# Moving key and value tiles to common places modulo 256, and weight sums forward in VectorE's order

## The chip, the core and the metric

The kernel runs on one core of a Trainium2 chip. The core has a matrix engine (TensorE, PE in the profile, with its weight loads as PEld), a vector engine (VectorE, DVE), an activation engine (ScalarE, ACT), GpSimd (POOL, nearly unused here) and a sync engine (SyncE, SP) that here issues almost all transfers between device memory and the on-chip memory. Engines run side by side; each takes its own instructions in the order in which they were written, and semaphores make one wait for another. The metric is the time of one execution on the device in microseconds (us), lower being better.

## The reference

Inputs are q, k and v, each [8 batches, 8 heads, 576 tokens, 64], and the weights of a channel mix. First attention, in chunks of 64 tokens:

```python
scores = scale * np.matmul(q_c, k_c.transpose(0, 1, 2, 4, 3))
scores = scores - np.max(scores, axis=-1, keepdims=True)
attn = np.exp(scores)
attn = attn / (np.sum(attn, axis=-1, keepdims=True) + 1e-09)
out = np.matmul(attn, v_c)
```

The heads are then laid side by side, which gives x, [8, 576, 512], and the channel mix follows (x_prev is x one token earlier, zero at the start of a batch):

```python
xk = mu_k * x + (1.0 - mu_k) * x_prev
xr = mu_r * x + (1.0 - mu_r) * x_prev
k = np.maximum(xk @ w_k, 0.0)
v = k * k @ w_v
r = 1.0 / (1.0 + np.exp(-(xr @ w_r)))
return (r * v).astype(np.float32)
```

w_k is 512 x 1024, w_v 1024 x 512, w_r 512 x 512.

## The kernel before

**Tiling.** The 8 x 576 = 4608 tokens are cut into 18 groups of 256. Groups 0 and 1, and the loading and splitting of the weights, are written out in START, one word per step; groups 2 to 17 follow the list GROUP, once per group g. Each matrix product of the channel mix is made from tensors split in a high and a low part, in three passes (high x high, high x low, low x high). In the texts three streams of matmuls are called after their steps:

- K (`moe_k`, L627; the matmul is at L636, tile pk): per group 4 blocks of 24 matmuls. The stationary tile is a 128x128 piece of w_k (wk0, wk1 for high and low), the moving tile 128x256 of xk (xkhi, xklo).
- R (`moe_r`, L682; L689, tile pr): 24 matmuls per group, stationary xr (xrhi, xrlo), moving 128x512 of w_r (wr0, wr1).
- V: up to group 3 `moe_v` (L708; L720, tile pv), stationary the squared activations kk, moving a quarter b of w_v, 128x256. From group 4 on `moe_halves` (L827; L910, tiles vx and vyz) makes the same in seven products of 12 matmuls in place of eight, with sums of quarters of w_v and sums of activations (ks); this needs the weight sums described below.

Beside these stand the small 64-wide matmuls of attention: scores (s, L1011), probabilities times values (xps, L1096), and the transposes of p (pt, L1078).

PE's order within a group from 4 on: K (4 blocks), pt, R, xps, the scores of the group after the next, V. Group 2 has scores ahead of its K and again at its end, so that the K of group 3 follows scores too; group 3 then has the order of the later groups.

**Attention for the next group** runs during K. On VectorE: maximum m (L1039), subtraction (L1045), the mix mr for R (L1158), the turns qT and kT (L386: 32x32 transposes of the loaded queries and keys of a later group, out of q_ring and k_ring), then sum z (L1052), two small steps, and the normalization of p (L1062), which pt on PE waits for. The exponential (L1048) is ScalarE's. Of the words of GROUP, `Sc` is this attention chain, `De` and `Dl` are the turns, `Mr`, `Md` and `Mk` the mixes, `Pq` the transposes and products with the values, `L4`, `Lm` and `Lv` the loads, `Z` and `H` the activation sums and their high parts, and `W` the seven products.

**The weight sums.** `split_weights` (L749) has in group 2 seven steps B.0 to B.6: B.0 takes two tiles of room (bs0, bs1) in the buffers that held the activations of an earlier group; B.1, B.2 and B.4 add the high and low parts of three quarters of w_v (128x1024, `total`), B.3, B.5 and B.6 subtract sums from each other (`less`). In group 3 B.0 and B.1 make one more sum and difference, and C.0, C.2 and C.4 copy three results to their high parts on ScalarE (L797), C.1, C.3 and C.5 make the low parts on VectorE (L801). Group 4 makes the fourth (E).

**Order.** Nothing is planned by a program: each word of START and GROUP issues its steps at its place, and so sets the order on every engine. A sign before a word limits it: `=` to group 2, `+` to the others, `!` and `~` to the last group or all but the last. A step already issued is passed over at a later word, so an unmarked word after an `=` word of the same name holds for the other groups alone.

**Loads.** SP issues the loads of q and k in pieces (L223), 16 for each of the two tensors and each half batch, then those of v (L201) and the stores of the output, all in one queue in the order of the words. In group 2 two half batches are loaded, after that one in some of the groups.

**Places.** On-chip tiles come from pools, which lie one behind the other in the order in which they are opened, from L110 on. All tiles of the large pools have a multiple of 256 bytes per partition, but the pools par (mu2), par_m (m) and par_z (z) have 64 bytes each, and the two x tiles 4160 each, so what stands behind them begins 64 later modulo 256 (128 behind both x tiles). Counted from the place of the identity tile (pool const, 512 bytes), the kernel before has, modulo 256: wr, xr (rp) and xk (kp) at 0, behind par_m wk and the quarters of w_v (wts) and one sum (tmp) at 64, behind par kk and ks (mx) at 128, behind par_z the rings, p, qT and kT (ld, att) at 192, and mo (which holds another of the sums) at 64.

Of the kernel before, what the change touches and what calls it, by code (L numbers as in the profile page):

```python
# [8 lines left out]
F32R = mybir.dt.float32r  # L9
# [7 lines left out]
P = 128  # L17
# [36 lines left out]


GROUP = """
=Nc.0 K0.0 =L4 Sc.0 Sc.1 K0.12 Mr.0 De.01 Lm Sc.2 K0.34 K1.0 K1.12 E.0 Mr.1 Sc.3456 Mr.2 K1.34 K2.0 K2.12 E.1 H.0 K2.34
K3.0 Pq.0 K3.12 Z.0 Pq.1 K3.34 Z.1 H.1 H.3 Z.2 H.4 Z.3 H.2 H.5 Z.456
R0.0 R1.0 Pq.2 +Nn.0 Lv Z.78 R0.1 R1.1 Pq.3 Pq.4 B.01 Md.0 Mk.0
V0 V1.0 W.0 W.1 W.2 !W.3 !W.4 W.5 W.6 W.7 Mk.1 C.0 C.2 C.4 W.8 B.2 Mk.2 B.3 =Dl.01 B.456 C.1 C.3 C.5 V1.12345678 W.9 W.10 W.12 W.11 ~W.3 ~W.4 W.13 W.14 W.15 W.16 =Nn.0  # L60
"""


# [18 lines left out]
def tile_chunk_attention_channel_mix(  # L82
# [13 lines left out]
    B_, H, S, D = q.shape  # L96
    DM, FF = w_k.shape
    w_k, w_v, w_r = (w.bitcast(I32) for w in (w_k, w_v, w_r))
    HP = H // 2
    NB = DM // P  # L100
# [6 lines left out]
    def pool(name, bufs=1):  # L107
        return ctx.enter_context(tc.tile_pool(name=name, bufs=bufs))

    const = pool("const")  # L110
    rp = pool("rp")
    kp = pool("kp")
    par_m = pool("par_m")
    wts = pool("wts")
    tmp = pool("tmp", 2)
    par = pool("par")
    mx = pool("mx")
    par_z = pool("par_z")
    ld = pool("ld")
# [133 lines left out]
        do(f_move, "A")  # L253


    wk = [wts.tile([P, NB, FF], F32R, name=f"wk{s}") for s in range(2)]
    wr = [rp.tile([P, NB, DM], F32R, name=f"wr{s}") for s in range(2)]
    HF, HD = NF // 2, DM // 2
    tok = slice(0, TT), slice(TT, G)
# [3 lines left out]
    B = {}  # L263
# [956 lines left out]
    with tc.manual_schedule():  # L1220
        for word in START.split():
            name, _, e = word.partition(":")
# [107 lines left out]
```

## Time and profile before

| what | value |
|---|---|
| median of three runs | 581.24 us (580.86 to 582.17) |
| profiled execution, its own time | 582.63 us |
| span of its instructions | 580.8 us |
| TensorE busy, share of the span | 570.2 us, 98% |
| VectorE busy | 456.7 us, 79% |
| ScalarE busy | 354.8 us, 61% |
| mean granted TensorE clock | 0.997 |
| one group in the middle (228.47 to 257.89) | 29.42 us |

Times in the profile count from the span's start; L636 is line 636 of the kernel. Matmuls are pipelined, so a single matmul's duration (281 ns) is longer than the step from one to the next; the paces in the texts are a stretch's length divided by its number of matmuls. The chain of waits follows the work that ended last back from the last instruction, at each step to what released it or to the instruction before it on the same engine; in order of time each row gives its start, its length and its work. In a timeline the bracket at the end of a row gives the engine's idle time before it and what ended it.

### The profile page before, as it was taken

To read this page: it belongs to the slowest core of one execution; us is meant where nothing else is said; L and a number is where in the kernel's file an instruction comes from. 1 tells how busy PE (TensorE), PEld (TensorE's weight loads), DVE (VectorE), ACT (ScalarE), POOL (GpSimd) and SP (SyncE) were. 2 spreads that over 40 slices of the span, in tenths; PEclk is the share of its full clock that TensorE was granted. 3 is DMA by queue.
4 is the path that set the end of the run, shared out by engine and by line. 5 is a ranking of instruction groups with operands and counts; after the bars stand their busy time and mean duration, and the time that the engine had idled before them with its cause. 6 is when DMAs were issued, how large, how long until landed. Compare 5 with 4: busy or idle time off the path is not lost.

```text
span 580.8 us, 15342 instructions
## 1 busy us (share of the span) xinstructions
PE 570.2 (98%) x6497; PEld 541.9 (93%) x6497; DVE 456.7 (79%) x753; ACT 354.8 (61%) x530; POOL 0.7 (0%) x6
## 2 busy tenths in 40 slices
PE   8899999999899999999999999999999999999997
PEld 7789999999799999999999999999999999999997
DVE  1699898749789788878887878888888787977835
ACT  4799875453639292929293838383847474747562
POOL 0000000000000000000000000000000000000000
PEclk9899999999999999999999999999999999999999
DMA  9997152443543434340234333344333311111011
GB/s 288 221 315 184 46 111 75 87 70 64 107 105 61 97 57 99 56 101 1 75 52 103 60 88 60 69 87 79 78 73 77 70 49 38 37 38 37 2 37 37
DMA packets 184276, 49.25 MB, mean 85 GB/s; under 512 B 169608, under 2 KB 176272, under 8 KB 184208
## 3 DMA queue, kind: packets, MB, share of 16 engines
q1 hardware_dynamic: 183904, 48.01, 36.5%
q8 instruction: 51, 0.84, 0.6%
q10 hardware_dynamic: 304, 0.27, 0.1%
q14 instruction: 17, 0.14, 0.1%
HBM read 38.80 MB, written 9.44 MB: 83 GB/s over the span
## 4 chain that ended last, share of the span: by engine, by line
PE 91%; DVE 3%; SPq 3%; ACT 1%; DMA 1%; issue 0%; DVEq 0%
PE pk L636 33%; PE pr L689 16%; PE vx L910 14%; PE vyz L910 10%; PE pv L720 6%; SPq L223 3%; PE xps L1096 3%; PE s L1011 2%; PE pt L1078 2%; PE warm L1225 1%; PE trq L367 1%; PE trk L367 1%; PE s L410 1%; PE mxk L580 1%; PE mxr L580 1%; DMA k_ring<-in_k 1%
## 5 line engine op out<-in xcount | busy, mean ns | idle before, releaser
L636 PE MATMUL pk<-xkhi,wk 128*128 128x256 f32 x1152 | 206.1, 281 | 0.0
L636 PEld LDWEIGHTS pk<-xkhi,wk 128*128 128x128 f32 x1152 | 178.4, 189 | 0.3
L636 PE MATMUL pk<-xklo,wk 128*128 128x256 f32 x576 | 161.4, 280 | 0.0
L636 PEld LDWEIGHTS pk<-xklo,wk 128*128 128x128 f32 x576 | 108.2, 188 | 0.1
L656 ACT ACTIVATE rr<-pk 128x512 f32<-128x512 f32 x56 | 33.0, 590 | 107.9 <-PE pk L636 107.7
L689 PE MATMUL pr<-wr,xrhi 128*128 128x512 f32 x288 | 90.4, 395 | 0.0
L910 PE MATMUL vx<-b,ks 128*128 128x256 f32 x504 | 64.0, 276 | 0.0
L910 PE MATMUL vyz<-b,kk 128*128 128x256 f32 x504 | 64.0, 276 | 0.0
L689 PEld LDWEIGHTS pr<-wr,xrhi 128*128 128x128 f32 x288 | 52.7, 188 | 10.2
L910 PEld LDWEIGHTS vx<-b,ks 128*128 128x128 f32 x504 | 60.3, 188 | 0.0
L910 PEld LDWEIGHTS vyz<-b,kk 128*128 128x128 f32 x504 | 60.2, 188 | 0.0
L689 PE MATMUL pr<-wr,xrlo 128*128 128x512 f32 x144 | 56.2, 390 | 0.0
L720 PE MATMUL pv<-b,kk 128*128 128x256 f32 x384 | 45.0, 277 | 0.0
L720 PEld LDWEIGHTS pv<-b,kk 128*128 128x128 f32 x384 | 44.1, 188 | 0.2
L939 ACT ACTIVATE u<-vx 128x256 f32<-128x256 f32 x28 | 10.8, 384 | 50.7 <-PE vx L910 50.7
L747 DVE TENSOR_TENSOR kk<-rr,kk 128x1024 fp32r<-128x1024 f32 x28 | 33.1, 1223 | 10.4 <-ACT kk L894 10.3
L747 DVE TENSOR_TENSOR xklo<-mk,xkhi 128x1024 fp32r<-128x1024 f32 x15 | 18.4, 1225 | 23.6 <-ACT xkhi L1168 23.6
L663 ACT ACTIVATE rr<-rr 128x512 f32<-128x512 f32 x56 | 35.4, 633 | 1.8
L689 PEld LDWEIGHTS pr<-wr,xrlo 128*128 128x128 f32 x144 | 27.0, 188 | 5.7
L1158 DVE SCALAR_TENSOR_TENSOR mk<-d,mu,x 128x256 f32<-128x256 f32 (+3 forms) x80 | 27.7, 413 | 0.4
L1158 DVE SCALAR_TENSOR_TENSOR mr<-d,mu,x 128x256 f32<-128x256 f32 (+3 forms) x80 | 27.6, 412 | 0.0
L856 DVE TENSOR_TENSOR ss<-rr 128x512 f32<-128x512 f32 x14 | 9.7, 692 | 21.8 <-ACT rr L663 21.8
(130 smaller groups left out, 885.5 us busy)
## 6 DMA issues: line engine op xcount, KB each, us to landing
v<-in_v SPq DMA_DIRECT2D x144, 64.0 KB, 2.4
out<-sg SPq DMA_DIRECT2D x34, 256.0 KB, 2.4
q_ring<-in_q SPq DMA_DIRECT2D x192, 36.0 KB, 2.0
k_ring<-in_k SPq DMA_DIRECT2D x192, 36.0 KB, 2.1
wk_st<-in_moe_w_k SPq DMA_DIRECT2D x4, 1024.0 KB, 12.7
wv_st<-in_moe_w_v SPq DMA_DIRECT2D x4, 1024.0 KB, 7.3
wr_st<-in_moe_w_r SPq DMA_DIRECT2D x2, 1024.0 KB, 10.0
q_ring<-in_q SPq DMA_DIRECT2D x2, 512.0 KB, 6.7
```

The costliest lines, as they stand in the source:

```text
L223: nc.sync.dma_start(out=ring[nm][pp : pp + 32, hp, a : a + n, :], in_=src[b, j * HP + hp, t0 : t0 + n * 32, dh * 32 : (dh + 1) * 32].rearr ...
L367: nc.tensor.matmul(x[halves[j], hp, :], T[f"{nm}{g}"][:, j * HP + hp, r, :], ident, start=True, stop=True,)
L580: nc.tensor.matmul(m[:, cb, s : s + w], diag[nm, n][:, cb], x[:, cb, c0 : c0 + w], start=(n == 0), stop=(n == 1),)
L636: nc.tensor.matmul(pk[:, e, :], wk[a][:, cb, f * P : (f + 1) * P], xk[b][:, cb, :], start=(n == 0), stop=(n == 3 * NB - 1),)
L656: nc.scalar.activation(r, T[f"pk{g}{fp}"], AF.Relu)
L663: nc.scalar.activation(r, r, AF.Square)
L689: nc.tensor.matmul(pr, xr[a][:, cb, tl * TT : (tl + 1) * TT], wr[b][:, cb, :], start=(n == 0), stop=(n == 3 * NB - 1),)
L720: nc.tensor.matmul(T[f"pv{g}{tl}"][:, cols[c]], kk[a][:, f, tok[tl]], quarter(f // HF, c)[:, b, f % HF, :], start=(f == 0 and n == 0 and c ...
L747: nc.vector.tensor_tensor(to, x, y, ALU.subtract)
L910: nc.tensor.matmul(to, a[i][:, f, :], weight(w, j, f), start=first and f == 0 and n == 0, stop=f == HF - 1 and n == 2, skip_group_check=True,)
L1096: nc.tensor.matmul(T[f"xps{g}"][halves[c], 2 * j + a, tl * TT + e * CH : tl * TT + (e + 1) * CH], T[f"v{2 * g + tl}"][halves[j], hp, e, :] ...
L1158: nc.vector.scalar_tensor_tensor(out=to[:, cb, s : s + w], in0=T[f"d{g}"][:, cb, s : s + w], scalar=mu[:, cb : cb + 1], in1=T[f"xg{g}"][:, ...
```

## The change

Two things. The pools are opened in another order: par stands first behind const, par_m moves behind tmp, and wk gets a pool of its own, wkp, between par_m and mx. In the same count as above, wr and xr come to lie at 64, xk at 64, the quarters and sums of w_v stay at 64, wk comes to 128, kk and ks stay at 128, and everything from par_z on stays where it was modulo 256.

| stream | stationary, moving before | stationary, moving after |
|---|---|---|
| K | wk 64, xk 0 | wk 128, xk 64 |
| V | kk or ks 128, weights 64 | kk or ks 128, weights 64 |
| R | xr 0, wr 0 | xr 64, wr 64 |

In GROUP, the weight sums of group 2 move forward: B.0 to B.2 behind the third K block's steps, B.3 to B.5 behind the x copy (Pq.4), B.6 behind the mix for K (Mk.0). In group 3 C.0 and C.1 move forward to the third K block, C.2 and C.4 behind Pq.4, C.3 and C.5 behind Mk.0. The number of instructions on each engine stays.

```diff
 GROUP = """
-=Nc.0 K0.0 =L4 Sc.0 Sc.1 K0.12 Mr.0 De.01 Lm Sc.2 K0.34 K1.0 K1.12 E.0 Mr.1 Sc.3456 Mr.2 K1.34 K2.0 K2.12 E.1 H.0 K2.34
+=Nc.0 K0.0 =L4 Sc.0 Sc.1 K0.12 Mr.0 De.01 Lm Sc.2 K0.34 K1.0 K1.12 E.0 Mr.1 Sc.3456 Mr.2 K1.34 K2.0 K2.12 E.1 H.0 K2.34 =B.012 C.01
 K3.0 Pq.0 K3.12 Z.0 Pq.1 K3.34 Z.1 H.1 H.3 Z.2 H.4 Z.3 H.2 H.5 Z.456
-R0.0 R1.0 Pq.2 +Nn.0 Lv Z.78 R0.1 R1.1 Pq.3 Pq.4 B.01 Md.0 Mk.0
-V0 V1.0 W.0 W.1 W.2 !W.3 !W.4 W.5 W.6 W.7 Mk.1 C.0 C.2 C.4 W.8 B.2 Mk.2 B.3 =Dl.01 B.456 C.1 C.3 C.5 V1.12345678 W.9 W.10 W.12 W.11 ~W.3 ~W.4 W.13 W.14 W.15 W.16 =Nn.0
+R0.0 R1.0 Pq.2 +Nn.0 Lv Z.78 R0.1 R1.1 Pq.3 Pq.4 C.24 =B.345 B.01 Md.0 Mk.0 =B.6 C.35
+V0 V1.0 W.0 W.1 W.2 !W.3 !W.4 W.5 W.6 W.7 Mk.1 W.8 Mk.2 =Dl.01 V1.12345678 W.9 W.10 W.12 W.11 ~W.3 ~W.4 W.13 W.14 W.15 W.16 =Nn.0
 """
...
     const = pool("const")
+    par = pool("par")
     rp = pool("rp")
     kp = pool("kp")
-    par_m = pool("par_m")
     wts = pool("wts")
     tmp = pool("tmp", 2)
-    par = pool("par")
+    par_m = pool("par_m")
+    wkp = pool("wkp")
     mx = pool("mx")
     par_z = pool("par_z")
...
-    wk = [wts.tile([P, NB, FF], F32R, name=f"wk{s}") for s in range(2)]
+    wk = [wkp.tile([P, NB, FF], F32R, name=f"wk{s}") for s in range(2)]
```

## The prediction

> **What bounds the kernel now.** I began with the busy time of each engine and the shares of the chain of waits by line.
>
> ```profile
> PE 570.2 (98%) x6497; PEld 541.9 (93%) x6497; DVE 456.7 (79%) x753; ACT 354.8 (61%) x530; POOL 0.7 (0%) x6
> PE pk L636 33%; PE pr L689 16%; PE vx L910 14%; PE vyz L910 10%; PE pv L720 6%; SPq L223 3%; PE xps L1096 3%; PE s L1011 2%; PE pt L1078 2%; PE warm L1225 1%; PE trq L367 1%; PE trk L367 1%; PE s L410 1%; PE mxk L580 1%; PE mxr L580 1%; DMA k_ring<-in_k 1%
> ```
>
> TensorE sets the time: its lines make nearly all of the chain. A wait elsewhere counts only where it stops PE, so two things are worth reading: how fast the matmul streams step, and where PE stands still. For the first, the chain in order of time (start, length, what; K is pk at L636, R is pr at L689, V is pv at L720 or vx and vyz at L910):
>
> ```profile
> 64.40 5.46 PE pr L689 x24
> 69.87 8.48 PE pk L636 x72
> 78.35 8.17 PE pv L720 x72
> ...
> 105.53 1.09 PE s L1011 x64
> 106.62 11.10 PE pk L636 x96
> ...
> 169.81 11.31 PE pk L636 x96
> ...
> 197.87 1.36 PE vx L910 x12
> 199.23 11.31 PE pk L636 x96
> ...
> 551.25 11.31 PE pk L636 x96
> 562.56 5.47 PE pr L689 x24
> 568.03 1.38 PE vx L910 x12
> ```
>
> K and V have one shape, a stationary 128x128 and a moving 128x256 tile, but not one pace. V steps by 1.36 / 12 = 113.3 ns; K from group 4 on by 11.31 / 96 = 117.8 ns. Yet K can step like V. The next rows are K's instructions alone in two stretches of 9 us (the number in brackets after PE's busy time counts its matmuls):
>
> ```profile
> 138.00:147.00 9.00, 9.00 (x82) 9.00 (x81) 1.00 0.38 75
> 171.00:180.00 9.00, 9.00 (x78) 9.00 (x78) 1.00 0.41 106
> ```
>
> PE is full in both at the full clock (the 1.00), with the same tiles at the same places; group 3 gets 82 matmuls through, group 4 78, 5% apart. So there are a quick pace and a slow pace, and what came before decides between them. K is quick where the 64-wide score matmuls (s) precede it, at 106.62, and slow where V precedes it without a break (the 14 blocks from 169.81 to 551.25, one a group), and where R does (69.87). V keeps its quick pace across seven products a group, though the product, the PSUM tile and the weights change at each: there the places modulo 256 stay. At V to K they change.
>
> The second thing, PE at rest, is in group 3. The same chain there, and VectorE's order just before it:
>
> ```profile
> 139.29 3.29 DMA k_ring<-in_k
> 142.67 1.67 DVE mr L1158 x4
> 144.33 1.16 DVE qT L386
> 145.49 1.13 DVE kT L386
> 147.19 1.14 DVE z L1052
> 148.85 1.24 DVE p L1062
> 150.13 1.09 PE pt L1078 x8
> ```
>
> ```profile
> 136.06 1.18 DVE L766 TENSOR_TENSOR bs<-b 128x1024 f32<-128x1024 f32 x1
> 137.27 2.49 DVE L747 TENSOR_TENSOR bs<-bs,bs 128x1024 f32<-128x1024 f32 x2
> 139.68 0.68 DVE L734 TENSOR_TENSOR sg<-pv,sg 128x512 f32<-128x512 f32 x1
> 140.28 1.21 DVE L1039 TENSOR_REDUCE m<-s 128x16 f32<-128x1024 f32 x1
> ```
>
> PE's last K matmul of group 3, and the same place in group 4, where nothing is late:
>
> ```profile
> 148.12 0.28 PE L636 MATMUL pk<-xkhi,wk 128*128 128x256 f32 x1
> ```
>
> ```profile
> 180.84 0.29 PE L636 MATMUL pk<-xkhi,wk 128*128 128x256 f32 x1
> 180.97 0.49 PE L1078 MATMUL pt<-ident,p 128*128 128x128 f32 x3
> ```
>
> In group 4 the transposes start 0.13 us after the last K matmul, in group 3 2.01 us after (150.13 - 148.12): 1.88 us of PE at rest, because VectorE normalizes p late. The maximum m needs only the scores, which PE makes just before K: K ends at 148.12 + 0.13 = 148.25 and takes 11.10 after scores (106.62), so they are done at 137.15. Three weight sums and an output scaling still stood in front of m then.
>
> **The change, part by part.** The execution profiled took 582.63 us (span 580.8), 1.39 above the median 581.24 of the three runs shown; the sum is a difference, taken from both.
>
> *Places.* Counted from the identity tile's place, the pools' sizes give, modulo 256: now K 64 stationary and 0 moving, V 128 and 64, R 0 and 0. Afterwards K and V are both 128 and 64, and R 64 and 64. The distance within K (64) and within R (0) stays. What goes is the change of place between V and K: the array sees V's pattern run on. I take it that K then stays in V's pace: 11.31 - 96 x 1.36 / 12 = 0.43 us a block, and 14 x 0.43 = 6.0 us. Bounds: 0, if the break at V to K has another cause, to 6.0; no loss, since no K row shows a pace below 118.
>
> If distance decides and not the place itself, two quick spells are lost. V at 78.35 steps by 8.17 / 72 = 113.5 ns though K before it was slow (8.48 / 72 = 117.8): the change of place brought it there, and will be gone. 72 x 4.3 ns = 0.31 us. The last V (84 matmuls from 568.03) is quick straight after R, with a place step of 128 for the stationary tile and 64 for the moving one; afterwards the step is today's from R to K, which leaves K slow at 69.87. 84 x 4.45 ns = 0.37 us. I count both as lost; bounds 0 and 0.68 together.
>
> R I leave at 5.47 / 24 = 228 ns: both operands share one place before and after. Bounds: the two paces of K differ by 4.45 ns, and 432 R matmuls at that are 1.9 us of gain; upward the slowest R row,
>
> ```profile
> 44.33 2.95 PE pr L689 x12
> ```
>
> is 246 ns, 18 ns more, or 7.8 us.
>
> A page of the Trainium skill speaks against this whole part: TensorE: Matmul & The Clock Gate (Part 2, What happens when you issue a matmul) gives PE two independent read ports and says that loading the next weights takes no read bandwidth from the running matmul. By that rule no placement could change the pace, and the 6.0 us would be 0. The two 9-us rows speak against its completeness, since one pair of tiles has two paces, but they don't name the cause; the rule has its own rival below.
>
> *Group 2's sums.* All seven steps (a reservation, six sums) move ahead on VectorE; none issues a DMA, and SP's order stays. Two sums go in before the last kk low part of K, three behind the x copy, one behind mk. Places with room, VectorE first and then ScalarE:
>
> ```profile
> 126.26 1.23 DVE L747 TENSOR_TENSOR d<-x 128x1024 f32<-128x1024 f32 x1 [3.90 <-ACT x L1122]
> ...
> 164.41 0.69 DVE L734 TENSOR_TENSOR sg<-pv,sg 128x512 f32<-128x512 f32 x1 [2.52 <-PE pv L720]
> ```
>
> ```profile
> 161.92 1.06 ACT L1168 ACTIVATE xkhi<-mk 128x1024 fp32r<-128x1024 f32 x1 [2.98 <-DVE mk L1158]
> ```
>
> Three sums are 3 x 1.22 = 3.7 us in VectorE's 3.90 us of waiting for x; without that cover each would delay x's difference by 1.2 us, which K needs only 137.15 - 126.26 = 11 us later. With them gone, m starts at about 137.25, when the scores end, and not at 140.28. What is late next? m and the subtraction take 142.67 - 140.28 = 2.39 and mr 1.66, so mr is done by 141.3, but the turns qT and kT stand ahead of z, and kT waits for the last keys to land at 139.29 + 3.29 = 142.58. That DMA is paced by SP's issues, which nothing here moves. So kT runs from 142.65 to about 143.8, not to 146.6. Then comes kk's low part, for which ScalarE must be done:
>
> ```profile
> 143.81 0.62 ACT L143 ACTIVATE kk<-relu 128x512 fp32r<-128x512 f32 x1
> ```
>
> That ends at 144.43; z follows 0.57 us later (146.62 to 147.19 now), and from z to the end of p it takes 148.85 + 1.24 - 147.19 = 2.90. So p is ready at 147.9, and PE wants it at 148.25. The 1.88 us go whole, with some 0.3 us to spare; bounds 0 (the landing a little later, or the turn's wait taking mr's place) to 1.88.
>
> *Group 3's splits.* C.3 and C.5 (2 x 1.22) go into VectorE's 2.52 us before the first scaling, C.2 and C.4 (two copies of the shape of xkhi's 1.06) into ScalarE's 2.98 us before xkhi, C.0 and C.1 beside K's end, where both engines wait for each other. Cost 0; uncovered they would delay xkhi and so K of group 4 by what exceeds these rests, under a microsecond.
>
> *Who covers the shorter K?* p must be normalized before K ends. The tightest group is 4:
>
> ```profile
> 179.07 1.23 DVE L1062 TENSOR_TENSOR p<-p,z 128x1024 f32<-128x1024 f32 x1
> ```
>
> It ends at 180.30 against 180.97. A K shorter by 0.43 leaves 0.24 us, so the gain reaches the end.
>
> **Sum.** 6.0 + 1.88 - 0.31 - 0.37 = 7.2 us: 582.63 becomes 575.4, and the median 581.24 becomes 574.0.
>
> **The rivals.**
>
> *The pace doesn't follow the places.* PE may lose its step at V to K for another reason (another weight matrix, another PSUM pool). For it: K is slow after R too (69.87). Against: V changes both at every product and keeps its pace. Then only the rest goes: 581.24 - 1.88 = 579.4. The Trainium skill's rule of two independent ports (TensorE: Matmul & The Clock Gate, Part 2) leads to the same time.
>
> *The keys land too late.* The wait for the DMA takes the place of the sums, and PE rests as long as now: 574.0 + 1.88 = 575.9. For it: the chain names this DMA. Against: VectorE had no rest between 142.67 and p's end.
>
> *Neither part does anything*: 581.2.
>
> *The other side: R pays.* R's 432 matmuls, whose two operands lie together, move to place 64, where K's stationary tile lies now while it is slow. If the place itself hurts and not the distance, K need not gain, and R at its slowest row costs 7.8: 581.24 - 1.88 + 7.8 = 587.2. It ends slower than before from (1.88 + 1.16) / 432 = 7 ns a matmul on. Against: V's moving tile has been at 64 all along, quick.
>
> *More than I count.* The early K and V blocks that are slow (24 + 72 + 24 + 18 = 138 matmuls, 0.6 us) come into step, the 0.68 isn't lost, and R gains its 1.9: 574.0 - 3.2 = 570.8.
>
> **How the numbers follow.** My forecast has 0.62, own range 573.3 (none of the 0.68 lost) to 574.9 (half of the 1.88 left); the unchanged pace 0.13; the late keys 0.08; neither 0.07; R pays 0.05; more 0.05. The range 572.6 to 579.8 holds the forecast, the late keys and the unchanged pace, 0.83. A difference of 0.2% (1.16 us) is about what three runs tell from none: faster 0.62 + 0.13 + 0.08 + 0.05 = 0.88, same 0.07, slower 0.05.
>
> **What would show it.** Right: the 14 K rows near 10.9 us and not 11.31; pt of group 3 starting within 0.2 us of the last K matmul; m of that group near 137.3; R still 5.47. Half right: K rows of 11.3, or a pt wait on p that stays. Wrong: R rows above 5.6, V rows above 1.40, or a new wait of PE in groups 4 to 17.

## The result and the profile after

The changed kernel takes 585.48 us (median of six runs, 584.55 to 586.69), the kernel before beside it 581.13 (580.85 to 582.64). The ratio is 1.007, with a 95% interval of 1.0051 to 1.0089: slower by 0.7%, where 574.0 had been forecast. The execution profiled took 586.23 us, its span is 584.5. The executions of one kernel fall into two sets about 2 us apart, here 584.55 to 584.81 at a mean granted clock of 0.999 or 1.000 and 586.16 to 586.69 at 0.997, so a kernel executed once is compared below only with executions at its own clock.

The busy line of the changed kernel's page:

```profile
PE 575.3 (98%) x6497; PEld 547.4 (94%) x6497; DVE 456.9 (78%) x753; ACT 354.3 (61%) x530; POOL 0.7 (0%) x6
```

PE is busy for 5.1 us more than before (575.3 against 570.2) with the same 6497 matmuls, and the rest of its span shrinks from 10.6 us to 9.2. So PE doesn't wait more; its matmuls step more slowly. The chain in order of time says which (start, length, work; lines after the change are one higher than before, so K is L637, R L690, V L721 and L911):

```profile
77.97 8.48 PE pv L721 x72
...
106.54 11.10 PE pk L637 x96
...
125.08 11.51 PE pv L721 x96
136.59 1.09 PE s L1012 x64
137.68 11.08 PE pk L637 x96
...
149.63 5.48 PE pr L690 x24
...
168.65 11.31 PE pk L637 x96
...
196.99 1.41 PE vx L911 x12
198.40 11.31 PE pk L637 x96
...
554.51 11.31 PE pk L637 x96
565.81 5.47 PE pr L690 x24
571.28 1.41 PE vx L911 x12
```

K behind V is 11.31 as before, in all 14 blocks; no gain there. V has lost its quick pace in every group from 2 on: a product takes 1.41 where it took 1.36 (117.5 ns a matmul, not 113.3, which within the rounding of the row is the 117.8 of K), the undivided V of groups 2 and 3 takes 11.51, and the early V at 77.97 takes 8.48 where the one at 78.35 took 8.17. K behind the scores (106.54, 137.68) is still quick. R still takes 5.47 or 5.48.

In group 3 the rest of PE is gone. VectorE there, and PE's last K matmul with the transposes behind it, as timelines of the changed kernel:

```profile
136.62 0.69 DVE L735 TENSOR_TENSOR sg<-pv,sg 128x512 f32<-128x512 f32 x1 [2.62 <-PE pv L721]
137.75 1.23 DVE L1040 TENSOR_REDUCE m<-s 128x16 f32<-128x1024 f32 x1 [0.43 <-PE s L1012]
...
142.89 1.20 DVE L387 STREAM_TRANSPOSE kT<-k_ring 128x1024 f32<-128x1024 f32 x1
...
147.18 1.22 DVE L1063 TENSOR_TENSOR p<-p,z 128x1024 f32<-128x1024 f32 x1
```

```profile
148.48 0.28 PE L637 MATMUL pk<-xkhi,wk 128*128 128x256 f32 x1
148.60 0.82 PE L1079 MATMUL pt<-ident,p 128*128 128x128 f32 x6
```

The maximum m starts at 137.75, 0.07 after the scores end (136.59 + 1.09 = 137.68). p is ready at 148.40, and pt starts at 148.60, 0.12 after the last K matmul. The sums' part of the change worked; the places' part cost more than it saved.

### The profile page after: what moved, and what is told of

Its sections match the earlier page's. It is cut to its first block, busy times and chain, and to the rows that moved or that the text cites. A ratio compares the mean times of both kernels' runs of the same rounds, so it can differ in the third digit from the quotient of the medians.

```text
span 584.5 us, 15341 instructions
## 1 busy us (share of the span) xinstructions
PE 575.3 (98%) x6497; PEld 547.4 (94%) x6497; DVE 456.9 (78%) x753; ACT 354.3 (61%) x530; POOL 0.7 (0%) x6
## 4 chain that ended last, share of the span: by engine, by line
PE 97%; DVE 2%; ACT 0%; issue 0%
PE pk L637 35%; PE pr L690 17%; PE vx L911 14%; PE vyz L911 10%; PE pv L721 8%; PE xps L1097 3%; PE s L1012 2%; PE pt L1079 2%; PE warm L1226 1%; PE trq L368 1%; PE trk L368 1%; PE s L411 1%; PE mxk L581 1%; PE mxr L581 1%; PE pt L475 0%; PE xps L495 0%
## 5 line engine op out<-in xcount | busy, mean ns | idle before, releaser
L637 PE MATMUL pk<-xkhi,wk 128*128 128x256 f32 x1152 | 206.4, 281 | 0.0
L637 PEld LDWEIGHTS pk<-xkhi,wk 128*128 128x128 f32 x1152 | 177.8, 189 | 0.3
L637 PE MATMUL pk<-xklo,wk 128*128 128x256 f32 x576 | 161.5, 280 | 0.0
L637 PEld LDWEIGHTS pk<-xklo,wk 128*128 128x128 f32 x576 | 108.3, 188 | 0.1
L657 ACT ACTIVATE rr<-pk 128x512 f32<-128x512 f32 x56 | 32.9, 588 | 113.3 <-PE pk L637 113.2
L690 PE MATMUL pr<-wr,xrhi 128*128 128x512 f32 x288 | 90.4, 395 | 0.0
L911 PE MATMUL vyz<-b,kk 128*128 128x256 f32 x504 | 66.2, 281 | 0.0
L911 PE MATMUL vx<-b,ks 128*128 128x256 f32 x504 | 66.2, 281 | 0.0
L911 PEld LDWEIGHTS vyz<-b,kk 128*128 128x128 f32 x504 | 62.4, 189 | 0.0
L911 PEld LDWEIGHTS vx<-b,ks 128*128 128x128 f32 x504 | 62.4, 189 | 0.0
L690 PEld LDWEIGHTS pr<-wr,xrhi 128*128 128x128 f32 x288 | 52.7, 188 | 10.1
L690 PE MATMUL pr<-wr,xrlo 128*128 128x512 f32 x144 | 56.1, 390 | 0.0
L721 PE MATMUL pv<-b,kk 128*128 128x256 f32 x384 | 46.2, 281 | 0.0
L721 PEld LDWEIGHTS pv<-b,kk 128*128 128x128 f32 x384 | 45.2, 189 | 0.2
L690 PEld LDWEIGHTS pr<-wr,xrlo 128*128 128x128 f32 x144 | 27.0, 188 | 5.7
```

The lines of the kernel that those rows point to most:

```text
L637: nc.tensor.matmul(pk[:, e, :], wk[a][:, cb, f * P : (f + 1) * P], xk[b][:, cb, :], start=(n == 0), stop=(n == 3 * NB - 1),)
L657: nc.scalar.activation(r, T[f"pk{g}{fp}"], AF.Relu)
L690: nc.tensor.matmul(pr, xr[a][:, cb, tl * TT : (tl + 1) * TT], wr[b][:, cb, :], start=(n == 0), stop=(n == 3 * NB - 1),)
L721: nc.tensor.matmul(T[f"pv{g}{tl}"][:, cols[c]], kk[a][:, f, tok[tl]], quarter(f // HF, c)[:, b, f % HF, :], start=(f == 0 and n == 0 and c ...
L911: nc.tensor.matmul(to, a[i][:, f, :], weight(w, j, f), start=first and f == 0 and n == 0, stop=f == HF - 1 and n == 2, skip_group_check=True,)
```

## The experiments

The theory on record is that a change of place between two streams changes their pace. The first rival is that each stream's pace comes from its own two places or the distance between them; the second that only the address far away counts (the weights of K moved by tens of thousands of bytes too); the third that no place matters. Places are again given modulo 256 as stationary/moving. The paces of a block of V from group 4 on are told by one product of 12 matmuls (1.36 or 1.41 us), those of K by its 96 (10.88 or 11.31). Ratios are against executions of the kernel before taken beside each run; where no ratio is given, the kernel was executed once and is read by its rows.

**The two parts one by one.** First the order alone, with the old places:

```diff
-=Nc.0 K0.0 ... H.0 K2.34
+=Nc.0 K0.0 ... H.0 K2.34 =B.012 C.01
...
-... Pq.4 B.01 Md.0 Mk.0
+... Pq.4 C.24 =B.345 B.01 Md.0 Mk.0 =B.6 C.35
```

> The order of the weight sums alone, the pools as before. If the two parts of the change are independent, as I hold: the rest of PE in group 3 goes (1.88 us, the transposes start within 0.2 us of the last K matmul), V stays at 113.3 ns and K at 117.8 ns, and the time falls by 1.9 us, to about 579.2 us. If the order itself had upset V's pace (because something now runs beside the start of V), V would be at 117.8 ns here too and the time about 585 us.

Measured: 579.53 us, ratio 0.9968 (0.9952 to 0.9984). The chain of waits of this run:

```profile
53.80 8.38 PE pk L636 x72
...
165.64 11.31 PE pk L636 x96
...
185.32 1.57 PE vx L910 x12
186.89 1.36 PE vyz L910 x12
```

The paces are those of before, and PE's rest in group 3 is gone. 0.32% of 581.98 is 1.9 us (0.9 to 2.8), against 1.88 in the forecast.

Then the places alone, with the old order:

```diff
     const = pool("const")
+    par = pool("par")
     rp = pool("rp")
     kp = pool("kp")
-    par_m = pool("par_m")
     wts = pool("wts")
     tmp = pool("tmp", 2)
-    par = pool("par")
+    par_m = pool("par_m")
+    wkp = pool("wkp")
...
-    wk = [wts.tile(
+    wk = [wkp.tile(
```

> The pools alone, the order as before. If the places alone set V's pace: V at 117.8 ns from group 2 on, K unchanged at 117.8 ns after V, the rest of PE in group 3 stays at about 1.9 us, and the time is about 587.3 us. If the order upsets V: the time of the kernel before, 581.1 us.

Measured: 587.47 us, ratio 1.0107 (1.0072 to 1.0142), V at 1.41 from group 4 on and K at 11.31. The two ratios multiplied give 1.0075, the whole change 1.007. All that is lost lies in the places. One detail differs: the last V, behind R, was quick here (its products take 1.36 or 1.37) and slow in the whole change, with the same places and the same order on PE.

**Far address or near place, and whose.** Next the weights of K went behind those of V, with no place modulo 256 changed: the quarters of w_v then lie exactly where the change puts them, the weights of K 64 bytes short of it. Then only the inputs moved (wr, xr and xk by 64), with the weights of K where they were:

```diff
     par = pool("par")
+    wkp = pool("wkp")
     mx = pool("mx")
...
-    wk = [wts.tile(
+    wk = [wkp.tile(
```

> The kernel before with one edit: wk gets its pool behind tmp, so that the quarters b of w_v move down by 32768 bytes to exactly where the change puts them, and wk up by 49152. No tile changes its place modulo 256 (K 64 and 0, V 128 and 64, R 0 and 0). Far-place theory (b and kk meet according to address bits above 256): V slow, 117.8 ns in every group, time about 587 us. Near-place theory (the places modulo 256 decide, those of the streams before V included): V quick, 113.3 ns, time about 581 us.

```diff
     const = pool("const")
+    par = pool("par")
     rp = pool("rp")
     kp = pool("kp")
-    par_m = pool("par_m")
     wts = pool("wts")
     tmp = pool("tmp", 2)
-    par = pool("par")
+    par_m = pool("par_m")
```

> The kernel before with the other half: par first and par_m behind tmp, so that wr, xr and xk move up by 64 bytes and wk, b, kk and ks stay where they were before. Modulo 256: K 64 and 64, R 64 and 64, V 128 and 64. Far-place theory: V quick, 113.3 ns; K may change, since its two tiles now share a place. Near-place theory: V slow as in the changed kernel, time about 587 us if K stays.

With the weights down: 580.66 us, ratio 0.9994 (0.9976 to 1.0013), every pace as before. The far address doesn't count. With the inputs up: 590.99 us, ratio 1.0168 (1.0139 to 1.0196): V slow although none of its tiles had moved, and K, with both tiles at 64, at 11.52 for 96 matmuls, 120.0 ns each, a third pace. So V's loss comes from the place of another stream's tiles, R's or K's.

**R's tiles or K's.** The runs up to the extra matmuls ahead of K stand on the order alone (579.53 us). First wr and xr at 64, the rest at the old places; then only xk at 64:

```diff
     const = pool("const")
-    rp = pool("rp")
     kp = pool("kp")
-    par_m = pool("par_m")
+    par = pool("par")
+    rp = pool("rp")
     wts = pool("wts")
     tmp = pool("tmp", 2)
-    par = pool("par")
+    par_m = pool("par_m")
```

> All four of these runs stand on the kernel of the order alone (579.5 us, V 113.3 ns, K 117.8 ns after V). Here only R's two tiles, wr and xr, move up by 64; K stays at 64 and 0, V at 128 and 64. If R's places decide how the V that follows two small streams later starts: V 117.8 ns as in the changed kernel, about 585.7 us. If K's places decide that: V stays at 113.3 ns, 579.5 us.

```diff
     rp = pool("rp")
+    par = pool("par")
     kp = pool("kp")
-    par_m = pool("par_m")
     wts = pool("wts")
     tmp = pool("tmp", 2)
-    par = pool("par")
+    par_m = pool("par_m")
```

> Only K's moving tile xk moves up by 64, so that K's two tiles share a place; R stays at 0 and 0. If R's places decide V's start: V 113.3 ns; K at 120 ns as in the run that moved all inputs up, about 582.6 us. If K's places decide it: V 117.8 ns, about 588 us.

The chain with R's tiles up:

```profile
178.86 5.49 PE pr L689 x24
...
187.98 1.41 PE vyz L910 x12
...
196.47 10.90 PE pk L636 x96
```

The chain with K's input up:

```profile
191.45 1.36 PE vyz L910 x12
...
199.61 11.52 PE pk L636 x96
```

It is R. With R at 64/64, R itself takes about as long as ever (5.49), V is slow, and K, at its old places 64/0 behind the slow V, is quick (10.90). That gain of K's was not expected, and so the 585.7 us expected for a slow V didn't come: 579.02 us were measured, at a clock of 1.000, where the order alone takes 578.35 to 578.60. What V loses K nearly gains back. With K's input up, V is quick and K at 120.0 ns, the slowest pace of K in any run. The 586.0 us are more than the 582.6 expected, in part because this execution had a clock of 0.997, and for the rest because K is that slow behind scores too (11.71 for 96, where it was 11.10) and the early K and V blocks are slower as well.

Does it take both of R's tiles? Once xr alone went to 64, once wr alone:

```diff
     const = pool("const")
-    rp = pool("rp")
+    wrp = pool("wrp")
     kp = pool("kp")
-    par_m = pool("par_m")
+    par = pool("par")
+    rp = pool("rp")
...
-    wr = [rp.tile(
+    wr = [wrp.tile(
```

> Only R's stationary tile xr moves up by 64: R's two tiles no longer share a place. If sharing a place costs a stream (K went from 117.8 to 120 ns when its tiles shared one): R falls from 227 ns by 2 ns or more, about 0.9 us in all, and if V keeps its pace the time is 578.6 us or less. If R is bound by its 512 columns and not by place: R 227 ns. V: quick if R's shared place is harmless to V whatever it is, slow if any move of R's tiles upsets it.

```diff
     rp = pool("rp")
     kp = pool("kp")
-    par_m = pool("par_m")
+    par = pool("par")
+    wrp = pool("wrp")
...
-    wr = [rp.tile(
+    wr = [wrp.tile(
```

> The order alone, and of the old places only R's moving weights move, from 0 to 64 (R's stationary inputs stay at 0). With both of R's tiles at 64 V was slow, with the stationary alone at 64 it was quick. If R's moving tile decides, V is slow here (9.88 us for the 84 products); if it is both tiles together, V is quick (9.52). R itself: near 235 ns as with the other tile moved, if the distance counts, near 232 otherwise. K is free to change, as it did before with R moved. Time 579 to 586.

The chain with xr alone at 64 (582.03 us, ratio 1.0006, 0.9973 to 1.0039), and then with wr alone (580.32 us):

```profile
180.54 5.60 PE pr L690 x24
...
189.75 1.36 PE vyz L911 x12
...
197.91 11.31 PE pk L637 x96
```

```profile
178.60 5.51 PE pr L690 x24
...
187.71 1.36 PE vyz L911 x12
...
195.88 11.31 PE pk L637 x96
```

V stays quick with either from group 2 on (the last V, with wr alone up, is slow: 1.41 a product). R itself is slower with its tiles apart: 0.13 us a group with xr moved, 0.04 with wr moved, which is 1.8 and 0.6 us over 14 groups. The expectation that R might gain 2 ns a matmul with its tiles apart is refuted: R's two tiles at one place cost R nothing. Of the three runs with tiles of R at 64, only that with both there upsets V in the groups from 2 on.

**Is the pace a property or a choice made at the start?** Ahead of K in groups 4 to 16 stood one extra matmul whose moving tile grows from group to group; its result is overwritten by the next, so no result changes and K starts otherwise than before:

```diff
             xk = T[f"xk{g}"]
+            many = (16, 32, 48, 64, 80, 96, 112, 128, 144, 160, 192, 224, 256, 0)[g - 4] if g >= 4 and fp == 0 else 0
+            if many:
+                nc.tensor.matmul(
+                    pk[:, 0, :many], wk[0][:, 0, 0:P], xk[0][:, 0, :many],
+                    start=True, stop=True, skip_group_check=True,
+                )
             for e in range(2):
```

> No place changes. Each K of groups 4 to 16 begins with one matmul more, whose result the first true one overwrites: the moving tile has 16, 32, 48, 64, 80, 96, 112, 128, 144, 160, 192, 224 and 256 columns in groups 4 to 16; group 17 has none. If the quick and the slow pace are two states of one stream, chosen by the offset between weight load and matmul at its start: for some of the sizes K runs at 113.3 ns from there on (10.9 us a group), for the others at 117.8. If the pace belongs to K's tiles after V: 117.8 ns in every group, and about 0.11 us more for each, 581 us.

The chain's K rows of groups 6, 7 and 11 (48, 64 and 128 columns):

```profile
224.49 11.39 PE pk L642 x96
254.03 10.98 PE pk L642 x96
...
370.50 11.36 PE pk L642 x96
```

The rows are up to 0.10 longer than without the extra matmul, but the two paces stand clear of each other: K is quick with 64, 80, 96, 112, 192 and 224 columns and slow with 16, 32, 48, 128, 144, 160 and 256 (577.61 us in all). The same tiles at the same places take either pace, for a whole block, by how the block starts. One size in all groups makes a kernel of it:

```diff
             xk = T[f"xk{g}"]
+            if g >= 4 and fp == 0:
+                nc.tensor.matmul(
+                    pk[:, 0, :80], wk[0][:, 0, 0:P], xk[0][:, 0, :80],
+                    start=True, stop=True, skip_group_check=True,
+                )
```

> The order alone (the old places), with an extra 80-column matmul ahead of K in groups 4 to 17, the size that made K quick in group 8 of the run with varied sizes. State theory: all 14 K blocks at 113.4 ns, each about 0.29 us shorter with the extra matmul counted, so 579.5 - 14 x 0.29 = 575.4 us, less than both kernels. If the quick K of that run hung on its group and not on the extra matmul's size, some groups stay at 117.7 and the time stays between 576 and 580.

Measured: 576.56 us (574.65 to 576.69), ratio 0.9904 (0.9877 to 0.993), and in each of the 14 groups the same row:

```profile
168.11 10.97 PE pk L641 x96
...
545.65 10.97 PE pk L641 x96
```

It is the size and not the group. One matmul more in each group makes the kernel faster than the kernel before and than the changed one.

**V's pace, and what K does behind it.** The same with the whole change: an extra matmul ahead of V, of the same sizes:

```diff
+            many = (16, 32, 48, 64, 80, 96, 112, 128, 144, 160, 192, 224, 256, 0)[g - 4]
+            if many:
+                nc.tensor.matmul(
+                    X()[:, :many], part(0, 0)[0][:, 0, :], weight(11, 0, 0)[:, :many],
+                    start=True, stop=True, skip_group_check=True,
+                )
             product(X(), part(0, 0), 11, True)
```

> The changed kernel with one extra matmul ahead of V in groups 4 to 16, of 16, 32, 48, 64, 80, 96, 112, 128, 144, 160, 192, 224 and 256 moving columns (its result is overwritten; group 17 has none). If V's slow pace in the changed kernel is a state chosen as the stream starts, some of the 13 blocks go back to 113.3 ns (the 84 fresh products then take 9.52 us and not 9.88) and the others stay at 117.8, as K did in the run with extra matmuls ahead of K. If it is a property of R's new place, all 13 stay at 117.8. K, which follows V, may change with it. Time by the state theory about 583 to 586; by the other 586 to 587.

The chain in group 8 (80 columns) and in group 12 (144):

```profile
309.53 1.36 PE vyz L911 x12
...
317.69 10.88 PE pk L637 x96
...
426.02 1.41 PE vyz L911 x12
...
434.50 11.31 PE pk L637 x96
```

V is quick with 80, 96, 112, 128, 192 and 224 columns and slow with the other seven, and K behind it has V's pace in all 13 groups: 10.88 behind a quick V, 11.31 behind a slow one (583.31 us). With K at V's places, K does take over V's pace. One size for all groups:

```diff
+            nc.tensor.matmul(
+                X()[:, :80], part(0, 0)[0][:, 0, :], weight(11, 0, 0)[:, :80],
+                start=True, stop=True, skip_group_check=True,
+            )
             product(X(), part(0, 0), 11, True)
```

> The changed kernel with an extra 80-column matmul ahead of V in groups 4 to 17. If R's place harmed V by the moment at which V starts and not by anything that lasts, all 14 V and all 14 K blocks are quick: a group is shorter by 29.76 - 29.12 = 0.64 us with the extra matmul counted, 585.5 - 14 x 0.64 = 576.5 us. If the quick groups of the earlier run hung on their predecessors, it stays between 578 and 586.

Measured: 578.01 us, ratio 0.9933 (0.9906 to 0.996). All V and K blocks from the extra matmul on are quick, but for the K of group 4, which follows the V of group 3, that has none:

```profile
167.19 11.31 PE pk L637 x96
...
188.54 1.36 PE vyz L911 x12
...
196.70 10.88 PE pk L637 x96
```

**The change with R left where it was.** If R alone stands between the change and its gain, one line is to be turned:

```diff
     const = pool("const")
-    par = pool("par")
     rp = pool("rp")
+    par = pool("par")
     kp = pool("kp")
```

> The changed kernel with one pool line moved: R's two tiles are back at place 0 and 0, K stays at V's places (stationary 128, moving 64), V as always. In every run so far with V at 128 and 64 and R's weights at place 0, V came quick out of the scores; in the changed kernel with an extra matmul ahead of V, K took over V's pace, quick or slow, in all 13 groups. If both hold, V is quick (9.52 us for the 84 fresh products, start to last) and K after it too (10.77 us for 96, not 11.19): 579.5 of the order alone less 14 x 0.42 = 573.6 us, below both kernels, and the forecast of 574.0 was right but for R. Rival: K's new place itself makes V or K slow: V 9.88 or K 11.19 stay and the time is 579 to 586.

Measured: 574.02 us (572.68 to 574.95), ratio 0.9875 (0.9848 to 0.9901). Its chain:

```profile
76.18 8.48 PE pv L721 x72
...
155.00 11.09 PE pv L721 x96
166.09 10.88 PE pk L637 x96
177.85 5.45 PE pr L690 x24
185.32 1.57 PE vx L911 x12
186.90 1.36 PE vyz L911 x12
...
195.06 10.88 PE pk L637 x96
...
566.26 1.37 PE vx L911 x12
```

V is quick, K behind it is quick, with no matmul added. This is the best of the kernels run: 1.25% below the kernel before, while the change as given is 0.7% above it, and 64 bytes of place of two tiles of R lie between them.

**The moment of R, or its address?** On the order alone, an extra matmul ahead of R in groups 4 to 16, so that R's start and length change and no place does:

```diff
+            many = (16, 32, 48, 64, 80, 96, 112, 128, 144, 160, 192, 224, 256, 0)[g - 4] if g >= 4 and tl == 0 else 0
+            if many:
+                nc.tensor.matmul(
+                    pr[:, :many], xr[0][:, 0, 0:TT], wr[0][:, 0, :many],
+                    start=True, stop=True, skip_group_check=True,
+                )
             n = 0
```

> The order alone with the old places, and one extra matmul ahead of R in groups 4 to 16, of 16, 32, 48, 64, 80, 96, 112, 128, 144, 160, 192, 224 and 256 moving columns (group 17 none). Between it and V stand R's 24 matmuls, 64 transposing and 64 score matmuls. If the moment at which R starts or ends reaches V's start through them, V is slow (9.88 us) in some of the 13 groups and quick (9.52) in others. If only R's address counts, V is quick in all 13. K after V stays at 117.8 ns wherever its start is unchanged.

V was quick in all 13 groups and K slow in all (579.6 us): R's start and length don't reach V. How its address does remains open. The table compares the run with R's tiles up and the run with K's input up; it gives the time from one matmul's start to another's between R and V in the trace, in ns, for groups 5 to 15:

```
                                    R at 64/64      R at 0/0, xk at 64
last R -> first xps                 318 or 319      318 or 319
last xps -> first s                 38 or 39        38 or 39
last s -> first V                   148 or 149      148 or 149
first V -> second V                 225 or 226      222 or 223
first V -> last V of 84             9880            9525
```

Up to V's first matmul the two agree within 1 ns, and so do the starts of the weight loads of V's first two matmuls (1 or 2 ns ahead of the first matmul, and 106 or 107 behind its start). The first step of V is 3 ns longer with R at 64/64, and 83 steps later V is 355 ns behind.

**Other distances.** All stationary tiles of the three streams at 128, then at 192, with all moving ones at 0 on the order alone (of V's moving tiles one, b1, stays at 64):

```diff
-    rp = pool("rp")
+    wrp = pool("wrp")
     kp = pool("kp")
-    par_m = pool("par_m")
     wts = pool("wts")
     tmp = pool("tmp", 2)
     par = pool("par")
+    par_m = pool("par_m")
+    rp = pool("rp")
+    wkp = pool("wkp")
     mx = pool("mx")
...
-    wk = [wts.tile(
-    wr = [rp.tile(
+    wk = [wkp.tile(
+    wr = [wrp.tile(
```

> The order of the changed kernel; all moving tiles of the three streams (K's xk, R's wr, V's b of the fresh and carried products) lie at place 0 modulo 256 and all stationary ones (wk, xr, kk, ks) at 128; one carried b stays at 64. Distances are thus 128 for all three, where before they were K 64, R 0, V 64. If the distance between a stream's two tiles decides the pace, all three streams get a pace that no run has shown yet for K and V, and the same one for both, whatever went before. If the pace is a state that is chosen as a stream starts, K and V stay at 113.3 or 117.8 ns and only which of the two changes. R at distance 64 took 235 ns and at distance 0 took 231.6: at 128 I expect 228 to 240, so at most 3.6 us more. Total between 574 (both quick) and 587 (both slow).

```diff
-    rp = pool("rp")
+    wrp = pool("wrp")
     kp = pool("kp")
-    par_m = pool("par_m")
     wts = pool("wts")
     tmp = pool("tmp", 2)
     par = pool("par")
+    par_m = pool("par_m")
+    par_z = pool("par_z")
+    rp = pool("rp")
+    wkp = pool("wkp")
     mx = pool("mx")
-    par_z = pool("par_z")
```

> As the run before, with all stationary tiles at 192 and the moving ones at 0. Distance theory: one pace for K and V, and by the run with K at distance 0 (120.0 ns) against 64 (113.3 or 117.8) it should differ from that of distance 128. State theory: again 113.3 or 117.8 ns, chosen at the start of each stream. Total between 574 and 587.

At 128: 591.84 us, ratio 1.0177 (1.0141 to 1.0214), above the 574 to 587 that were expected. At 192: 587.53 us, ratio 1.0103 (1.007 to 1.0136). The chain at 128, with the product of group 4 that reads b1 and the K block behind, and then a K block at 192:

```profile
197.42 1.36 PE vx L912 x12
...
201.63 11.39 PE pk L638 x96
```

```profile
198.10 11.31 PE pk L638 x96
```

Distance 128 brings a fourth pace, 118.7 ns for K, and the products of V take 1.42 or 1.43; only the one that reads b1, and whose two tiles so lie 64 apart, takes 1.36 here and 1.39 in the later groups. At 192 K and V have the known slow pace (11.31 and mostly 1.41). So the distance bears on the pace, and the expectation that only the two known paces occur failed for 128. But the distance alone doesn't settle it: one distance, 64, has two paces.

## Why the prediction was wrong, and where it was right

**Where the paces went.** The table gives the paces in the kernel before, in the changed one and in the runs that part its causes (V from group 4 on, without the last V; K behind V):

| kernel | R | K | V's pace | K's pace behind it |
|---|---|---|---|---|
| before, order alone | 0/0 | 64/0 | quick | slow |
| changed | 64/64 | 128/64 | slow | slow |
| changed, R back | 0/0 | 128/64 | quick | quick |
| R's tiles up | 64/64 | 64/0 | slow | quick |
| xr up, or wr up | 64/0, 0/64 | 64/0 | quick | slow |
| xk up | 0/0 | 64/64 | quick | 120.0 ns |
| inputs up | 64/64 | 64/64 | slow | 120.0 ns |

**K stays in V's pace: right.** "I take it that K then stays in V's pace" holds in every group of every run with K at V's places: 14 with both slow, 14 with both quick with R back, 6 and 7 with the extra matmul ahead of V. The term's size was right too: 11.31 - 10.88 = 0.43 a block, 14 blocks, 6.0 us, in the kernel with R back.

From V to K the change of place turns the pace over, as assumed: from group 4 on, K at 64/0 is slow straight behind a quick V and quick straight behind a slow one. From K to V it need not. The prediction says of the quick early V behind a slow K that "the change of place brought it there"; with R's tiles up, K and that V have the same places as before, and the V is slow:

```profile
67.89 8.48 PE pk L636 x72
76.38 8.48 PE pv L720 x72
```

The same two lengths stand in the run with wr alone up.

**V keeps its pace: the step that failed.** It was never written as a term. The sum took V's 113.3 ns as given in the groups, because V's own places don't change, and asked of R's move only what R itself would pay ("R I leave at 5.47 / 24 = 228 ns"; it is 5.45 to 5.48). What R's place does to V behind it was not asked, although two steps away the prediction counted such losses itself: "If distance decides and not the place itself, two quick spells are lost". The bound "no loss, since no K row shows a pace below 118" is the same gap: it bounds K, and the loss came in V. In the changed kernel K follows a slow V and gains nothing, and V loses. The losses by rows are these. 13 blocks at (1.61 + 6 x 1.41) - (1.57 + 6 x 1.36) = 0.34 are 4.4 us (1.57 as in the order alone), those of groups 2 and 3 (11.51 against the 11.09 of the run with R back) 0.84, together 5.3; the forecast's 0.31 for the early V came (8.48 for 8.17), and the last V lost 7 x (1.41 - 1.36) = 0.35, where 0.37 was forecast; the K at 55.34 took 8.68 where the order alone has 8.38, another 0.30. That is +6.2, less 1.88 for the sums +4.3; the medians differ by 4.35. The two executions profiled differ by less, 586.23 - 582.63 = 3.60, because the changed one reached that K 0.68 earlier (55.34 for 56.02); its start varies from execution to execution.

That the last V's loss came is no proof of the reason given for it, a step of place from R. The places alone left this V quick, and in the run with the extra matmuls ahead of K, whose last group has none and whose places are the old ones, it is slow:

```profile
562.63 1.41 PE vx L916 x12
```

**The sums: right.** m starts when the scores end, the keys' landing stopped nothing (kT runs at 142.89 right behind the other turn), p is ready 0.20 us ahead of pt where some 0.3 was forecast. 1.88 was counted, 1.9 measured with the order alone. The splits of group 3 cost nothing that the chain shows.

**The tightest group**, 4, covered the shorter K: the kernel with R back has the whole 0.43 in its rows from 166.09 on, and pt follows K at 166.09 + 10.88 = 176.97 without a wait.

**With R back the forecast is met:** 574.02 us against 574.0. That it agrees so closely is partly luck: of the two lost spells only one was lost there (8.48 at 76.18, but 1.37 at the end), and the ratio's interval, 0.9848 to 0.9901 of 582.12, is 573.3 to 576.4.

**The rivals.** "R pays" (587.2) came nearest in time and is wrong in its mechanism: it put the price into R's rows, which stay, and the argument against it, that V's moving tile at 64 was quick all along, says nothing about R's effect on V. "The pace doesn't follow the places" is refuted by the one pool line between 585.48 and 574.02. "What would show it" had the right sign to look for, V rows above 1.40, without a case that priced it.

The Trainium skill (TensorE: Matmul & The Clock Gate, Part 2, What happens when you issue a matmul) gives PE two independent read ports and says that loading the next weights takes no read bandwidth from the running matmul; taken alone, that would give all K and V blocks one pace. The runs show four for one shape, 113.3, 117.8, 118.7 and 120.0 ns, by place and by start. The measurement decides: the rule alone doesn't tell the pace of these streams. Whether the read ports are where the difference arises, no run here shows.

## What to carry to other kernels

When one stream of matmuls of one shape has two paces in a profile, look at what precedes it as well as at where its tiles lie: a pace can be handed on from stream to stream, and a tile that is moved must be priced for the streams behind its own too. Move one tile at a time and read each stream's rows, since a gain in one and a loss in the other can stand in the same total (R's tiles up: V slow, K quick, 579.02 us against 578.35 to 578.60 at the same clock). Where the start decides, a short dummy matmul ahead of the stream is a cheap probe of that, and here it paid for itself (576.56 us).

## What the runs showed of the hardware

- A stream of 128x256 matmuls whose two tiles lie 64 bytes apart modulo 256, and in which PE never stops, runs as a whole block at 113.3 or at 117.8 ns a step with the same tiles; 16 columns more or less in one matmul ahead of it (48 or 64, 112 or 128 for K) decide which.
- Its two tiles at one place modulo 256 give 120.0 ns where K was so placed, and 118.7 for K at distance 128. R, whose moving tile has 512 columns, is quickest with its tiles at one place (5.45 to 5.49 us for 24) and takes 5.51 to 5.60 with one of them 64 away.
- R's place reaches V across 128 small matmuls, within which the trace shows no difference above 1 ns. R's length and start do not. By what it reaches V is not settled, nor is why the last V, straight behind R, was quick with the places alone and slow with the whole change, and slow with the old places in the run with extra matmuls ahead of K.
